# Top-k attention and a mixer MLP on one core: the distance to a candidate threshold as whole numbers, and weights that load later

## The chip, the cores and the metric

The kernel runs on one core of a Trainium2 chip. The time is the device time of one execution in microseconds (us). A core has five engines that run side by side, each through its own list of instructions in order: TensorE (PE, matrix products), VectorE (DVE), ScalarE (ACT), GpSimd (POOL) and SyncE (SP, which here only issues transfers). They wait for each other through semaphores. Sixteen DMA engines carry the transfers.

## The reference

```python
# q, k, v: (8, 8, 576, 64) float32;  x: (8, 576, 512)
scores = scale * np.matmul(q, k.transpose(0, 1, 3, 2))          # 576 x 576 per head
kth = np.partition(scores, -32, axis=-1)[..., -32:-31]          # 32nd largest of each row
scores = np.where(scores >= kth, scores, -1e9)
attn = softmax(scores);  attn_out = np.matmul(attn, v)
x = attn_out.transpose(0, 2, 1, 3).reshape(B, S, H * D)
h = np.maximum(x.transpose(0, 2, 1) @ w_tok1, 0.0) @ w_tok2     # token mixing, 576 -> 256 -> 576
u = x + h.transpose(0, 2, 1)
out = u + np.maximum(u @ w_ch1, 0.0) @ w_ch2                    # channel mixing, 512 -> 1536 -> 512
```

So each of 36,864 rows needs its own threshold, the 32nd largest of 576 scores, before its softmax.

## The kernel before

**Tiling.** Two heads make a pair; there are 32 pairs, four to a batch. The 576 rows of a head are four blocks of 128 and a rest of 64. For each pair, four groups `g` hold one block of both heads (two row tiles, `n == 2`), and a fifth group holds the two rests as one row tile. That gives 9 row tiles for a pair, 36 for a batch and 288 in all. Line numbers are those of the kernel before.

**One group.** Q and K are loaded by SyncE, transposed on TensorE (L369, L371) and copied out by ScalarE (L377, L380). Then:

1. TensorE multiplies the scores into PSUM (L399, L391); ScalarE copies them to `Sb` in SBUF (L429, L432).
2. VectorE takes the eight largest of each of seven segments of a row into `cd` (L442). Two rounds of maximum and replacement drop 16 values (L447 to L452), and the last maximum (L454) gives `thi`, whose eighth value is a candidate: at least 24 scores of the row are at or above it, in most rows exactly 24.
3. ScalarE's sign operation (L455) compares all 576 scores with the candidate, writes the signs to `sg`, and sums them into `cnt`, which tells the candidate's rank.
4. GpSimd multiplies scores and signs into `X` (L461): scores at or above the candidate become negative, those below stay positive. Eight dummy columns behind the 576 (L464, from `kdum` and `cnt`) stand for the places that the rank leaves, large or small, so that the eighth largest of the 584 columns is the threshold whatever the rank is between 24 and 31.
5. VectorE takes that maximum (L469, `tlo`), GpSimd negates its eighth value (L472, `nt`).
6. For groups of two, GpSimd writes the mask `U` as steep bytes from `Sb` and `nt` (L478). TensorE computes the scores a second time (L409) and adds the mask through the identity (L414); ScalarE's exponential writes `Pm` (L483). The single tile goes through `E`, `M` and a product on GpSimd instead (L488 to L493).
7. SyncE issues a DMA transpose `PT` (L497). When a pair's five groups have theirs and `vb`, V cast to bf16 by GpSimd (L382), is there, TensorE multiplies by V (L514, L518), and VectorE normalises into `Xb` (L530 to L539).

**MLP.** When a batch's four pairs are normalised, TensorE runs the MLP of that batch (first L562, then L580 to L589, L606, L627, L631) with copies on ScalarE (L569, L595, L612, L638). It runs between the attention of the next batch; the last batch's stands alone at the end.

**Order.** A planner in the kernel's source, `Plan`, writes every engine's order when the program is built. Each step is added with its engine, a duration and a due time; due times come from `T` (the spacing of row tiles) and the offsets `DUE`. A step is taken when its inputs, a free buffer and its engine are there in the planner's own account, no more than `AHEAD` before it is due. The order is then fixed: an engine that waits for one instruction does not pass to the next. Loads of weights are steps of GpSimd (`weight`, L307), which issues those transfers; all other transfers are issued by SyncE.

**Guard.** At the end `judge` (L662) tests counts and thresholds on VectorE; where a test fails, an exact version of the whole computation follows.

Of the kernel before, what the change touches and what calls it, by code (L numbers as in the profile page):

```python
# [8 lines left out]
P = 128  # L9
TOPK = 32  # L10
NEG = -1.0e30
LOW = -(2.0**100)
CUT = 8396807.0 / 8388608.0
NSEG = 7
RANK_BASE = 24
NDUM = 8
SHRINK = 2.0**-20
STEEP = -(2.0**100)
DROP = 2.0**-100
BELOW = -(1.0 - 2.0**-24)  # L20
FLOOR = 2.0**-66
# [3 lines left out]
T = 2.4326  # L25
DUE = dict(
    lq=30.233, tq=-12.175, ck=20.425, vc=11.748, mm=-33.047, cp=-28.9818283514137, seg=23.504, rnd=-2.208,
    sg=37.023, x=39.168, dum=4.693, mx=25.934, nt=-6.127, u=-3.8878283514136998, re=10.162, ex=-7.834,
    ex1=-1.811, tr=-27.916, pv=44.427, nm=-12.844, mlp=20.353,
# [10 lines left out]
class Op:  # L40
    __slots__ = ("eng", "dur", "due", "fn", "deps", "acq", "use", "lat", "n", "start", "end", "kids", "wait", "ready", "dma")


class Plan:
    LAT = {"DVE": 0.14, "ACT": 0.15, "POOL": 0.11, "PE": 0.13, "SP": 0.05}
    AHEAD = 87.6
# [8 lines left out]
    def add(self, eng, dur, due, fn, deps=(), acq=(), use=(), lat=None, dma=0.0):  # L55
# [5 lines left out]
        o.dma = dma  # L61
        o.n, o.kids = len(self.ops), []
# [27 lines left out]
    def run(self):  # L90
# [3 lines left out]
        for o in self.ops:  # L94
            o.wait, o.ready = len(o.deps), 0.0
# [87 lines left out]
def kernel(  # L183
# [14 lines left out]
    i32 = mybir.dt.int32  # L198
    u8 = mybir.dt.uint8
# [38 lines left out]
    lift = sbt("lift", [P, 1], f32)  # L238
    kdum = sbt("kdum", [P, NDUM], f32)
# [7 lines left out]
    tlo = sbt("tlo", [P, NT, 8], f32)  # L247
# [7 lines left out]
    slots("Sb", 5, [P, 2, S], f32)  # L255
# [3 lines left out]
    slots("sg", 4, [P, S], bf16)  # L259
    slots("X", 3, [P, 2, XW], f32)  # L260
# [4 lines left out]
    slots("PT", 9, [P, 10, P], bf16)  # L265
# [23 lines left out]
    for j in range(NDUM):  # L289
        nc.vector.memset(kdum[:, j : j + 1], float(S - 2 * RANK_BASE + 1 - 2 * (j + 1)))  # L290
# [10 lines left out]
    nc.vector.memset(lift[:, :], LIFT)  # L301
    for t in Xbs:
        nc.vector.memset(t[:, 4, :], 0.0)
# [3 lines left out]
    def weight(key, at, lat, f):  # L307
        wl.setdefault(key, []).append(plan.add("POOL", 1.0, at, f, lat=lat))
# [19 lines left out]
    def pair_ops(p):  # L328
# [6 lines left out]
        def ld_main(buf, src):  # L335
            for h in range(2):
                nc.sync.dma_start(
# [11 lines left out]
        def ld_kv(buf, src):  # L349
            def f():  # L350
                ld_main(buf, src)
                nc.sync.dma_start(
# [6 lines left out]
        lq = plan.add("SP", 0.24, tl, ld_q, acq=[qL], dma=1.4)  # L359
        lk = plan.add("SP", 0.2, tl + 0.1, ld_kv(kL, k), acq=[kL], dma=1.4)  # L360
        lv = plan.add("SP", 0.2, tl + 0.2, ld_kv(vL, v), acq=[vL], dma=1.4)
# [3 lines left out]
        def tr(buf, src, n):  # L365
# [11 lines left out]
        eq = plan.add("ACT", 0.62, t0 + DUE["ck"], lambda: nc.scalar.activation(  # L377
            out=qT.t[:, :], in_=pq.t[0][:, pq.t[1] : pq.t[1] + PW], func=AF.Copy, scale=SHRINK),
# [39 lines left out]
        for g in range(5):  # L418
# [17 lines left out]
            sgn, xs, mxs = [], [], []  # L436
            for h in range(n):
                i = i0 + h
                cd, m8, sg = Buf("cd"), Buf("m8"), Buf("sg")
                ss = []  # L440
                for a in range(NSEG):
# [13 lines left out]
                sgn.append(plan.add("ACT", 0.82, t + DUE["sg"] + 0.8 * h, lambda i=i, h=h, sg=sg, Sb=Sb: nc.scalar.activation(  # L455
                    out=sg.t[:, :], in_=Sb.t[:, h, :], func=AF.Sign, scale=-CUT, bias=thi[:, i, 7:8],
                    accum_out=cnt[:, i : i + 1]), [a5], acq=[sg], use=[Sb], lat=0.17))
                xs.append((i, h, sg))
            xo = []
            for i, h, sg in xs:  # L460
                xo.append(plan.add("POOL", 1.26, t + DUE["x"] + 1.4 * h, lambda h=h, sg=sg, Sb=Sb, X=X: nc.gpsimd.tensor_tensor(  # L461
                    out=X.t[:, h, 0:S], in0=Sb.t[:, h, :], in1=sg.t[:, :], op=ALU.mult),
                    [sgn[h]], acq=[X] if h == 0 else [], use=[Sb, sg, X]))
            dm = plan.add("POOL", 0.20, t + DUE["dum"], lambda n=n, i0=i0, X=X: nc.gpsimd.tensor_tensor(  # L464
                out=X.t[:, 0:n, S:XW], in0=kdum[:, :].unsqueeze(1).to_broadcast([P, n, NDUM]),
                in1=cnt[:, i0 : i0 + n].unsqueeze(2).to_broadcast([P, n, NDUM]), op=ALU.subtract),
                [xo[0]] + sgn, use=[X])
            for i, h, sg in xs:
                mxs.append(plan.add("DVE", 0.69, t + DUE["mx"] + 1.2 * h, lambda i=i, h=h, X=X: nc.vector.max(  # L469
                    tlo[:, i, :], X.t[:, h, :]), [dm, xo[h]], use=[X]))  # L470
            lasts.extend(mxs)
            on = plan.add("POOL", 0.27, t + DUE["nt"], lambda n=n, i0=i0, nt=nt: nc.gpsimd.tensor_scalar(  # L472
                out=nt.t[:, 0:n], in0=tlo[:, i0 : i0 + n, 7], scalar1=-1.0 if n == 2 else BELOW,
                scalar2=None, op0=ALU.mult), mxs, acq=[nt])
            if n == 2:
                us = []
                for i, h, sg in xs:
# [404 lines left out]
```

## Time and profile before

| | |
|---|---|
| median of 3 runs | 851.89 us (851.38 to 853.02) |
| the profiled execution, its own time | 854.5 us |
| its span, first to last instruction | 852.6 us |
| busy: PE, DVE, ACT, POOL | 772.0, 745.8, 680.8, 709.4 us |
| mean granted TensorE clock | 0.978 |

A row of instructions in the profile gives line, engine, operation, output and input with their shapes, the count, the busy time in us and the mean of one in ns, and then how long the engine stood idle just before them and for whom. A row of a stretch of time gives, for each engine, its busy time in that stretch and, in brackets, the number of instructions; then the granted TensorE clock as a share of full speed, the DMA engines' share and GB/s. A row of waits names who waited for whom: us in total, times, the longest. A row of a timeline gives the start and the length in us, and at its end the idle time before it with what released it. A row of DMA issues ends with the median time from issue to landing.

### The profile page before, as it was taken

The page shows a single profiled execution, that of the slowest core. Times are in us where ns is not written, and L with a number is a line of the kernel's source. Part 1 is how long each engine was busy: PE and PEld are TensorE (multiplying, and loading weights), DVE is VectorE, ACT ScalarE, POOL GpSimd, SP SyncE. Part 2 cuts the span into 40 slices and gives each one's busy share as a digit, 9 for nine tenths or more (in the row PEclk, how much of TensorE's full clock was granted, in tenths as well). Part 3 has the DMA queues.
Part 4 walks back from the last instruction along what each step waited for, and adds up shares of the span by engine and source line. Part 5 has one row for each costly group of instructions (what it writes and reads, how often), then busy time and mean ns, then how long its engine had stood idle before and what let it go on. Part 6 is the DMA issues. An engine that isn't in the chain of part 4 may idle for free.

```text
span 852.6 us, 20703 instructions
## 1 busy us (share of the span) xinstructions
PE 772.0 (91%) x6188; PEld 499.9 (59%) x6226; DVE 745.8 (87%) x4527; ACT 680.8 (80%) x1121; POOL 709.4 (83%) x978
## 2 busy tenths in 40 slices
PE   2467777999999999999999999999999999999995
PEld 1334445666566755676567755676567755676562
DVE  4499999999989998999989998999989998999700
ACT  1477777988789988899789988899789988898451
POOL 3299998999998999899988999899988999899500
PEclk9879988999999999999999999999999999999999
DMA  8945455456465555745486556755475555532701
GB/s 153 175 76 101 97 109 106 91 111 87 112 144 96 104 104 131 136 84 104 101 148 101 104 107 136 128 84 104 100 147 103 105 105 135 88 61 49 142 2 60
DMA packets 313017, 90.16 MB, mean 106 GB/s; under 512 B 305728, under 2 KB 307648, under 8 KB 312896
## 3 DMA queue, kind: packets, MB, share of 16 engines
q1 hardware_dynamic: 310144, 84.98, 51.5%
q0 software_dynamic: 2752, 3.77, 2.7%
q8 instruction: 51, 0.84, 0.4%
q14 instruction: 70, 0.57, 0.2%
HBM read 35.85 MB, written 9.44 MB: 53 GB/s over the span
## 4 chain that ended last, share of the span: by engine, by line
PE 52%; DVE 24%; POOL 8%; ACT 7%; issue 3%; DMA 3%; SPq 1%; ACTq 0%; POOLq 0%; DVEq 0%
PE bank L627 12%; PE bank L409 10%; DVE cd L442 9%; PE bank L399 7%; DVE tlo L469 7%; PE bank L606 6%; PE bank L414 5%; POOL X L461 3%; ACT Sb L429 3%; PE bank L514 3%; PE bank L369 2%; PE bank L391 2%; POOL U L478 2%; DMA vL<-in_v_dram 2%; ACT sg L455 2%
## 5 line engine op out<-in xcount | busy, mean ns | idle before, releaser
L442 DVE MAX8 cd<-Sb 128x8 f32<-128x82 f32 (+1 forms) x2016 | 393.0, 231 | 28.5 <-ACT Sb L429 28.2
L461 POOL TENSOR_TENSOR X<-Sb,sg 128x576 f32<-128x576 f32 x288 | 364.7, 1280 | 4.1 <-ACT sg L455 3.1
L455 ACT ACTIVATE sg<-Sb,thi 128x576 bf16<-128x576 f32 x288 | 222.8, 775 | 49.1 <-DVE thi L454 46.1
L469 DVE MAX8 tlo<-X 128x8 f32<-128x584 f32 x288 | 218.9, 761 | 21.8 <-POOL X L464 15.7
L478 POOL TENSOR_SCALAR U<-Sb,nt 128x576 uint8<-128x576 f32 x256 | 191.3, 747 | 23.8
L399 PE MATMUL bank<-kT,qT 64*128 64x288 f32 x1024 | 159.6, 438 | 24.7 <-ACT kT L380 13.4
L409 PE MATMUL bank<-kT,qT 64*128 64x288 f32 x1024 | 162.9, 437 | 7.8 <-ACT Sb L429 3.4
L483 ACT ACTIVATE Pm<-bank 128x1152 bf16<-128x1152 f32 x128 | 143.9, 1125 | 25.4 <-PE bank L414 21.0
L429 ACT COPY Sb<-bank 128x1152 f32<-128x1152 f32 x128 | 141.1, 1111 | 23.2 <-PE bank L399 20.8
L399 PEld LDWEIGHTS bank<-kT,qT 64*128 64x128 f32 x1024 | 91.9, 191 | 62.8 <-ACT Sb L429 15.7
L409 PEld LDWEIGHTS bank<-kT,qT 64*128 64x128 f32 x1024 | 93.9, 192 | 55.9 <-ACT Sb L429 11.2
L627 PE MATMUL bank<-wc2b,H 128*128 128x512 bf16 (+1 forms) x457 | 111.9, 380 | 2.8 <-issue 1.0
L606 PE MATMUL bank<-UT,wc1b 128*128 128x288 bf16 x768 | 104.3, 286 | 1.5 <-ACT UT L595 0.8
L414 PE MATMUL bank<-U,identN 128*128 128x288 bf16 x512 | 86.8, 292 | 10.5 <-POOL U L478 10.5
L606 PEld LDWEIGHTS <-wc1b 128*128 128x128 bf16 x768 | 73.5, 98 | 24.0 <-issue 5.0
L414 PEld LDWEIGHTS <-identN 128*128 128x128 bf16 x512 | 40.1, 98 | 69.0 <-issue 61.2
L627 PEld LDWEIGHTS <-H 128*128 128x128 bf16 (+1 forms) x480 | 45.3, 100 | 52.3 <-issue 8.2
L612 ACT ACTIVATE H<-bank 128x576 bf16<-128x576 f32 x96 | 61.6, 649 | 9.4 <-PE bank L606 7.8
L454 DVE MAX8 thi<-cd 128x8 f32<-128x56 f32 x288 | 58.5, 203 | 0.6
L455 ACT ACTIVATION_READ_ACCUMULATOR sg<-Sb,thi 128x1 f32 x288 | 55.6, 193 | 0.0
L450 DVE MAX8 m<-cd 128x8 f32<-128x35 f32 x288 | 52.6, 183 | 1.3
L452 DVE MATCH_REPLACE8 cd<-m,cd 128x35 f32<-128x35 f32 x288 | 52.6, 182 | 0.0
(85 smaller groups left out, 905.9 us busy)
## 6 DMA issues: line engine op xcount, KB each, us to landing
qL<-in_q_dram SPq DMA_DIRECT2D x64, 128.0 KB, 2.9
kL<-in_k_dram SPq DMA_DIRECT2D x64, 128.0 KB, 2.8
vL<-in_v_dram SPq DMA_DIRECT2D x64, 128.0 KB, 2.9
out_dram<-ob SPq DMA_DIRECT2D x16, 512.0 KB, 3.2
PT<-Pm SPq DMA_TRANSPOSE x160, 3.4
wc1b<-in_moe_w_ch_dram POOLq DMA_DIRECT2D x4, 384.0 KB, 9.0
wc2b<-in_moe_w_ch_dram POOLq DMA_DIRECT2D x4, 384.0 KB, 8.4
qL<-in_q_dram SPq DMA_DIRECT2D x64, 16.0 KB, 2.3
```

The lines of the kernel that those rows point to most:

```text
L399: nc.tensor.matmul(out=o[:, h, i, :], lhsT=qT.t[r, g * P : (g + 1) * P], rhs=kT.t[r, i * HS : (i + 1) * HS], start=True, stop=True)
L409: nc.tensor.matmul(out=o[:, h, i, :], lhsT=qT.t[r, g * P : (g + 1) * P], rhs=kT.t[r, i * HS : (i + 1) * HS], start=True, stop=False)
L414: nc.tensor.matmul(out=o[:, h, i, :], lhsT=identN[:, :], rhs=um[:, h, i * HS : (i + 1) * HS, 0], start=False, stop=True)
L429: nc.scalar.copy(out=Sb.t[:, :, :].rearrange("p h (a b) -> p h a b", a=2), in_=pairs(s1.t))
L442: ss.append(plan.add("DVE", 0.146, t + DUE["seg"] + 1.0 * h, lambda a=a, h=h, cd=cd, Sb=Sb: nc.vector.max(cd.t[:, a, :], Sb.t[:, h, bounds ...
L455: sgn.append(plan.add("ACT", 0.82, t + DUE["sg"] + 0.8 * h, lambda i=i, h=h, sg=sg, Sb=Sb: nc.scalar.activation(out=sg.t[:, :], in_=Sb.t[: ...
L461: xo.append(plan.add("POOL", 1.26, t + DUE["x"] + 1.4 * h, lambda h=h, sg=sg, Sb=Sb, X=X: nc.gpsimd.tensor_tensor(out=X.t[:, h, 0:S], in0= ...
L469: mxs.append(plan.add("DVE", 0.69, t + DUE["mx"] + 1.2 * h, lambda i=i, h=h, X=X: nc.vector.max(tlo[:, i, :], X.t[:, h, :]), [dm, xo[h]], ...
L478: us.append(plan.add("POOL", 0.80, t + DUE["u"] + 0.01 * h, lambda h=h, nt=nt, U=U, Sb=Sb: nc.gpsimd.tensor_scalar(out=U.t[:, h, :, 1], in ...
L483: oe = plan.add("ACT", 1.08, t + DUE["ex"], lambda s2=s2, Pm=Pm: nc.scalar.activation(out=Pm.t[:, :, 0:S].rearrange("p h (a b) -> p h a b" ...
L606: nc.tensor.matmul(out=o[:, i, :], lhsT=wc1b[:, cc, fc * P : (fc + 1) * P], rhs=UT.t[:, cc, i * HS : (i + 1) * HS], start=(cc == 0), stop= ...
L627: nc.tensor.matmul(out=po, lhsT=H2.t[:, fc, cs], rhs=wc2b[:, fc, :], start=(fc == 0), stop=False)
```

## The change

- `X` is now 32-bit whole numbers: score minus candidate, times `GRID` (2^34), by one scalar operation on GpSimd that reads `Sb` and the candidate. Scores below the candidate become negative.
- VectorE reads `X` as unsigned words, in which the negative numbers are the largest, so its maximum picks the scores next below the candidate.
- The sign now reads `X` and so comes after it, and writes one scratch tile `sg` instead of one of four; its sum `cnt` has the other sign, so `kdum` has too. The dummies of each row tile are an operation of their own.
- The masks are written from `X` instead of `Sb`. `Sb` has four buffers instead of five, `X` five instead of three, `PT` eight instead of nine.
- Q is no longer scaled when it is copied.
- A weight load is not planned before its due time (`nb`). K of the first pair is loaded through ScalarE's queue.
- The planner's durations, offsets, `T` and `AHEAD` are others, so all orders are written anew; the guard's tests are put in terms of the new numbers.

```diff
-T = 2.4326
+T = 2.3874
 DUE = dict(
...
-    AHEAD = 87.6
+    AHEAD = 196.0
...
-            o.wait, o.ready = len(o.deps), 0.0
+            o.wait, o.ready = len(o.deps), o.nb
...
-    slots("Sb", 5, [P, 2, S], f32)
+    slots("Sb", 4, [P, 2, S], f32)
...
-    slots("sg", 4, [P, S], bf16)
-    slots("X", 3, [P, 2, XW], f32)
+    sg = sbt("sg", [P, S], bf16)
+    slots("X", 5, [P, 2, XW], i32)
...
-    slots("PT", 9, [P, 10, P], bf16)
+    slots("PT", 8, [P, 10, P], bf16)
...
-        wl.setdefault(key, []).append(plan.add("POOL", 1.0, at, f, lat=lat))
+        wl.setdefault(key, []).append(plan.add("POOL", 0.6, at, f, lat=lat, nb=at))
...
-        lq = plan.add("SP", 0.24, tl, ld_q, acq=[qL], dma=1.4)
-        lk = plan.add("SP", 0.2, tl + 0.1, ld_kv(kL, k), acq=[kL], dma=1.4)
+        lq = plan.add("SP", 2.6, tl, ld_q, acq=[qL], dma=0.9)
+        lk = plan.add("SP", 1.9, tl + 0.1, ld_kv(kL, k, nc.scalar if p == 0 else nc.sync), acq=[kL], dma=0.9)
...
-                sgn.append(plan.add("ACT", 0.82, t + DUE["sg"] + 0.8 * h, lambda i=i, h=h, sg=sg, Sb=Sb: nc.scalar.activation(
-                    out=sg.t[:, :], in_=Sb.t[:, h, :], func=AF.Sign, scale=-CUT, bias=thi[:, i, 7:8],
-                    accum_out=cnt[:, i : i + 1]), [a5], acq=[sg], use=[Sb], lat=0.17))
...
-                xo.append(plan.add("POOL", 1.26, t + DUE["x"] + 1.4 * h, lambda h=h, sg=sg, Sb=Sb, X=X: nc.gpsimd.tensor_tensor(
-                    out=X.t[:, h, 0:S], in0=Sb.t[:, h, :], in1=sg.t[:, :], op=ALU.mult),
-                    [sgn[h]], acq=[X] if h == 0 else [], use=[Sb, sg, X]))
-            dm = plan.add("POOL", 0.20, t + DUE["dum"], lambda n=n, i0=i0, X=X: nc.gpsimd.tensor_tensor(
-                out=X.t[:, 0:n, S:XW], in0=kdum[:, :].unsqueeze(1).to_broadcast([P, n, NDUM]),
-                in1=cnt[:, i0 : i0 + n].unsqueeze(2).to_broadcast([P, n, NDUM]), op=ALU.subtract),
-                [xo[0]] + sgn, use=[X])
...
+                xo.append(plan.add("POOL", 0.77, t + DUE["x"] + 0.8 * h, lambda i=i, h=h, Sb=Sb, X=X: nc.gpsimd.tensor_scalar(
+                    out=X.t[:, h, 0:S], in0=Sb.t[:, h, :], scalar1=thi[:, i, 7:8], scalar2=GRID,
+                    op0=ALU.subtract, op1=ALU.mult), [a5], acq=[X] if h == 0 else [], use=[Sb, X]))
+                sgn.append(plan.add("ACT", 0.76, t + DUE["sg"] + 0.8 * h, lambda i=i, h=h, X=X: nc.scalar.activation(
+                    out=sg[:, :], in_=X.t[:, h, 0:S], func=AF.Sign, scale=1.0, bias=half[:, :],
+                    accum_out=cnt[:, i : i + 1]), [xo[h]], use=[X], lat=0.17))
+            for h in range(n):
+                dm = plan.add("POOL", 0.20, t + DUE["dum"] + 0.8 * h, lambda i=i0 + h, h=h, X=X: nc.gpsimd.tensor_scalar(
+                    out=X.t[:, h, S:XW], in0=kdum[:, :], scalar1=cnt[:, i : i + 1], scalar2=None,
+                    op0=ALU.subtract), [sgn[h]], use=[X])
+                mxs.append(plan.add("DVE", 0.69, t + DUE["mx"] + 1.2 * h, lambda i=i0 + h, h=h, X=X: nc.vector.max(
+                    tlo[:, i, :], X.t[:, h, :].bitcast(u32)), [dm, xo[h]], use=[X]))
...
-                    us.append(plan.add("POOL", 0.80, t + DUE["u"] + 0.01 * h, lambda h=h, nt=nt, U=U, Sb=Sb: nc.gpsimd.tensor_scalar(
-                        out=U.t[:, h, :, 1], in0=Sb.t[:, h, :], scalar1=nt.t[:, h : h + 1], scalar2=STEEP,
+                    us.append(plan.add("POOL", 0.80, t + DUE["u"] + 0.01 * h, lambda h=h, nt=nt, U=U, X=X: nc.gpsimd.tensor_scalar(
+                        out=U.t[:, h, :, 1], in0=X.t[:, h, 0:S], scalar1=nt.t[:, h : h + 1], scalar2=STEEP,
```

More of the change, by code (lines that the diff above doesn't have):

```diff
@@ L61, in add @@
         o.dma = dma
+        o.nb = nb
         o.n, o.kids = len(self.ops), []
@@ L198 @@
     i32 = mybir.dt.int32
+    u32 = mybir.dt.uint32
     u8 = mybir.dt.uint8
@@ L246 @@
     thi = sbt("thi", [P, NT, 8], f32)
-    tlo = sbt("tlo", [P, NT, 8], f32)
+    tlo = sbt("tlo", [P, NT, 8], u32)
+    tli = tlo.bitcast(i32)
     qLs = slots("qL", 2, [P, 5, 2, D], f32)
@@ L471, in pair_ops @@
             lasts.extend(mxs)
[L472 to L474 removed]
+            on = plan.add("POOL", 0.30, t + DUE["nt"], lambda n=n, i0=i0, nt=nt: nc.gpsimd.tensor_scalar(
+                out=nt.t[:, 0:n], in0=tli[:, i0 : i0 + n, 7], scalar1=-1.0,
+                scalar2=SLACK, op0=ALU.mult, op1=ALU.add), mxs, acq=[nt])
```

81 lines of the change are left out of this document (37 added, 44 removed).

## The prediction, made before the changed kernel ran

> **What bounds the kernel now.** I read the page's busy shares first, then the busy time of each engine stage by stage, and only then the waits. The page gives one execution:
>
> ```profile
> span 852.6 us, 20703 instructions
> PE 772.0 (91%) x6188; PEld 499.9 (59%) x6226; DVE 745.8 (87%) x4527; ACT 680.8 (80%) x1121; POOL 709.4 (83%) x978
> ```
>
> Four engines are above 80%, so the shares alone decide nothing. I cut the span at the first matmul of a batch's MLP (L562), because that is where TensorE gets a second kind of work. These rows show the cuts: the first MLP, the second, the seventh and the eighth.
>
> ```profile
> 148.30 0.22 PE bank L562
> ...
> L562 PE MATMUL bank<-Xb,w1b x9: 379/379/379, 254.3 to 256.3; 128*128 128x512 bf16 x9
> ...
> L562 PE MATMUL bank<-Xb,w1b x9: 379/379/379, 734.3 to 736.2; 128*128 128x512 bf16 x9
> ...
> 809.62 2.32 PE L562 MATMUL bank<-Xb,w1b 128*128 128x512 bf16 x9 [1.09 <-DVE Xb L532]
> ```
>
> The table of stages, with those cuts (the sixth row is one of the five equal periods between 254.3 and 734.3):
>
> ```profile
> core 0: us, PE busy (x) PEld busy (x) DVE busy (x) ACT busy (x) POOL busy (x), PEclk, DMA share, GB/s
> 22.70:50.00 27.30, 11.91 (x62) 7.45 (x60) 16.06 (x117) 13.31 (x23) 12.84 (x17) 0.75 0.80 140
> 50.00:100.00 50.00, 38.96 (x304) 24.24 (x300) 49.38 (x309) 39.46 (x66) 47.09 (x65) 0.93 0.56 103
> 100.00:148.30 48.30, 35.02 (x270) 22.10 (x268) 44.94 (x277) 35.57 (x59) 43.34 (x61) 0.86 0.51 100
> 148.30:254.30 106.00, 101.70 (x818) 65.83 (x821) 100.45 (x608) 92.68 (x152) 99.52 (x136) 1.00 0.56 109
> 638.30:734.20 95.90, 94.41 (x775) 61.43 (x779) 91.08 (x562) 84.70 (x141) 87.66 (x121) 1.00 0.57 113
> 734.30:809.60 75.30, 73.49 (x635) 48.40 (x638) 68.31 (x383) 58.65 (x97) 60.90 (x85) 1.00 0.43 81
> 809.60:852.60 43.00, 32.38 (x221) 20.39 (x223) 1.21 (x5) 13.98 (x20) 0.00 (x0) 0.95 0.09 30
> ```
>
> The reader should see three regimes. Stage A, up to 148.3, is attention alone: TensorE is idle a quarter of the time and VectorE carries it (49.38 of 50). From 148.3 on TensorE is busy 94.41 of every 95.9 us, at a granted clock of 1.00: it bounds the periods, with 1.5 us to spare, and VectorE (91.08) is close behind. The last 43.0 us are the last MLP. GpSimd, which the change relieves most, bounds no stage: it has 8 us to spare per period.
>
> **The fill.** Where VectorE stood still in stage A, and what stood behind it:
>
> ```profile
> DVE tlo L469 <- POOL X L464: 11.4, 2, 11.2
> DVE cd L442 <- ACT Sb L429: 9.7, 1, 9.7
> ```
>
> ```profile
> 12.47 0.55 DVE L303 MEMSET Xb<- 128x256 uint32 x2
> 17.07 1.09 PE L369 MATMUL bank<-identF,kL 128*128 128x128 f32 x4 [9.09 <-DMA kL<-in_k_dram]
> 22.68 1.27 DVE L442 MAX8 cd<-Sb 128x8 f32<-128x82 f32 x8 [9.66 <-ACT Sb L429]
> 31.11 0.72 POOL L382 TENSOR_SCALAR vb<-vL 128x640 bf16<-128x640 f32 x1 [9.78 <-DMA vL<-in_v_dram]
> 40.25 0.72 POOL L382 TENSOR_SCALAR vb<-vL 128x640 bf16<-128x640 f32 x1 [5.57 <-DMA vL<-in_v_dram]
> ```
>
> ```profile
> q0 software_dynamic: 1008, 1.80, 51.7%
> kL<-in_k_dram SPq DMA_DIRECT2D x4, 128.0 KB, 7.5
> vL<-in_v_dram SPq DMA_DIRECT2D x3, 128.0 KB, 12.0
> ```
>
> ```profile
> kL<-in_k_dram SPq DMA_DIRECT2D x64, 128.0 KB, 2.8
> vL<-in_v_dram SPq DMA_DIRECT2D x64, 128.0 KB, 2.9
> 0.74 1.36 SPq L337 DMA_DIRECT2D qL<-in_q_dram  x2
> ```
>
> In the first 20 us the weights (q0) take 51.7% of the DMA engines, and K and V need 7.5 and 12.0 us to land where 2.8 and 2.9 are the medians of the whole run. VectorE is through its memsets at 13.02 and waits for scores until 22.68. Then GpSimd stands at the V casts until 40.25 with the dummies (L464) queued behind it, and VectorE loses 11.2 us more.
>
> **Part by part.** The weights leave the start: in the new written order the first weight load stands behind the fourth X operation of GpSimd and the last behind the thirty-fifth. Pair 0's K goes to ScalarE's queue. Each issue takes 0.68 us (1.36 for two), so its three are out by 2.8 and, at 2.8 to 7.5 us, land at 5.6 to 10.3. From K's first transpose to VectorE's first maximum the rows give 22.68 - 17.07 = 5.6 us: 11.2 to 15.9. The memsets (one more, of one column) end at about 13.1, so VectorE starts at 13.1 to 15.9; I take 13.1, since the load of the DMA engines that made 7.5 is gone. The Trainium skill ("DMA: Bandwidth & Descriptors", "Issuing engines are not separate DMA queues") speaks against the move to ScalarE's queue: it saves issue time only. By it alone K would be out on SyncE at 5.4, land at 8.2, and the start be 13.8: the sum would be 0.7 worse. No run shows it yet.
>
> The V casts stay on GpSimd's path. SyncE's sixteenth issue (pair 1's V) ends at 0.74 + 16 x 0.68 = 11.6 and lands at 14.5; GpSimd needs it after two X, near 16. Its twenty-sixth (pair 2's V) lands at 18.4 + 2.9 = 21.3, behind the fifth X, near 22. So the 11.2 goes. If V still needs 12.0, the third lands at 30.4 and some 9 us of stall stay.
>
> Stage A also holds one tile's first part less: VectorE's written order has 44.7 row tiles' segments before the fourth normalisation, where before it had 45.7, and 40 last maxima in both. A tile is 91.08 / 36 = 2.53 us, of which the last maximum takes 0.76, so 1.77 for the rest.
>
> ```profile
> L461 POOL TENSOR_TENSOR X<-Sb,sg 128x576 f32<-128x576 f32 x288 | 364.7, 1280 | 4.1 <-ACT sg L455 3.1
> L469 DVE MAX8 tlo<-X 128x8 f32<-128x584 f32 x288 | 218.9, 761 | 21.8 <-POOL X L464 15.7
> L478 POOL TENSOR_SCALAR U<-Sb,nt 128x576 uint8<-128x576 f32 x256 | 191.3, 747 | 23.8
> L464 POOL TENSOR_TENSOR X<-kdum,cnt 128x16 f32<-128x16 f32 (+1 forms) x160 | 34.4, 215 | 12.1 <-ACT sg L455 4.6
> ```
>
> Stage A after: 13.1 + (148.3 - 22.7) - 11.2 - 1.8 = 125.7, **22.6 us earlier**. Bounds: 25 earlier if VectorE's other idle time shrinks too; 10.8 earlier if it starts at 15.9 and 9 us of stall stay.
>
> GpSimd's own saving: X becomes one scalar operation with one tile read. The nearest row is the mask (747 ns; same width, scalar operand per row); the far end is the old 1280. At 747 a period saves 36 x 0.533 = 19.2 us, and pays 16 more dummy operations x 0.215 = 3.4: GpSimd goes from 87.66 to 71.9. That is worth nothing directly, since TensorE ends the periods. Twelve weight issues move between the X operations; at most 9.4 us in all, hidden by that slack:
>
> ```profile
> L311 POOL DMA_DIRECT2D wc2b<-in_moe_w_ch_dram x4 | 3.1, 780 | 0.0
> ```
>
> The sign moves behind X, on ScalarE. It now writes one scratch tile, so each sign waits for the one before; behind it in ScalarE's queue are the copies out of PSUM, for which TensorE waits. What is lost is this overlap:
>
> ```profile
> 29.38 0.19 ACT L455 ACTIVATION_READ_ACCUMULATOR sg<-Sb,thi 128x1 f32 x1
> 29.47 0.76 ACT L455 ACTIVATE sg<-Sb,thi 128x576 bf16<-128x576 f32 x1
> ```
>
> The second sign starts 0.10 before the first one's sum is read out (29.57). Lost 36 times a period, that is 3.6 us: ScalarE 84.70 to 88.3 of 95.9. I charge TensorE 0.4 of it per period, bounds 0 and 3.6. The Trainium skill ("ScalarE: Activation LUTs", "What ACT_TABLE_LOAD costs") says that back-to-back activations overlap by about 93 ns, which this row agrees with; by that figure 288 signs would cost 27 us if all of it lay on the path, which is the slower rival below. VectorE's maximum over unsigned words I leave at 761 (+0 to +0.1). The scaling of Q and the checks at the end change no count that matters.
>
> Stage B (148.3 to 254.3): TensorE's written order has 27, 50, 70 ... 160 score blocks before the eight MLPs in both kernels, so its work stays 101.70. VectorE's falls: 35.3 tiles begun and 37 finished, before 39.3 and 42: 4 x 1.77 + 5 x 0.76 = 10.9 less, 89.6. So TensorE with the periods' idle ends it: 101.7 + 1.5 = 103.2; I take 103.5, **2.5 earlier** (0 to 4.3).
>
> Five periods: 480.0 + 5 x 0.4: **2 later** (7.5 earlier, with no idle left, to 10 later).
>
> Stage D (734.3 to 809.6): those tiles come back. VectorE has 27 tiles to begin and 29 to finish, before 22.7 and 27: 4.3 x 1.77 + 2 x 0.76 = 9.1 more, 77.4 against 75.3. So at least 2.1 later, at most 9.1; **I take 4**, as 7 us of its idle time are there to fill. The last MLP stays at 43.0.
>
> Sum: -22.6 - 2.5 + 2 + 4 = -19.1. The profiled execution took 854.5 (852.6 of span), which becomes 835.4; the median of the runs, 851.89, becomes **832.8**.
>
> **The rivals.** *GpSimd still stands at V*: the loads' rate, not the weights, sets V's landing. Then A gains 10.8: 844.6. For it: the loads of three pairs still stand in a row on SyncE. Against: 51.7% of the DMA time was the weights'. 0.12. *TensorE reaches its floor*: with GpSimd's slack every period is 94.4: 2 + 7.5 less, 823.3; 0.10. *X is no cheaper*: the conversion holds it at 1280 ns; GpSimd is at 87.66 + 3.4 = 91.1 a period, which still fits, but its masks come later; at 1 us a period 840; 0.05. *Slower, through ScalarE*: the sign waits for GpSimd and for the sign before it, with the PSUM copies queued behind it. If none of the 3.6 is hidden, 6.8 periods from B to D pay 24.5 instead of the 2: 855.3. It decides from 3.0 us a period, where the 20 us gained are spent. For it: ScalarE's 11 us of slack are in small pieces. Against: the copies have TensorE's own pace to hide in. 0.12. *Slower, through VectorE*: unsigned words cost 0.1 per maximum, 3.6 a period, VectorE 94.7 against TensorE's 94.4; nearly all 8 batches pay: 860; 0.03.
>
> **How the numbers follow.** My forecast has 0.58. The bounds of A, C and D taken together reach from 817 to 860; 819 to 851 leaves out the two slower cases and little else. What a measurement of this kernel can tell from no change is 0.2%, 1.7 us. Faster: 0.58 + 0.10 + most of 0.12 and 0.05 = 0.83; the same 0.02; slower 0.15.
>
> **What would show it.** Right: VectorE's first maximum near 13, no wait of 11 us at the dummies, X near 750 ns, the first L562 near 126, periods of 96, and the stretch from the seventh to the eighth MLP near 79. Wrong: a first L562 after 138 (the V casts), periods over 97 with ScalarE's copies late (the signs), a last maximum over 0.8 us.

## The result, and the profile after

The changed kernel takes **1240.34 us** (median of 4 runs, 1239.87 to 1241.34), the kernel before 851.63 us (849.22 to 853.02) beside it: ratio 1.457, 95% interval 1.4535 to 1.4605. The prediction said 832.8 us, 819 to 851. It was wrong in sign and by some 400 us.

The page of the changed kernel, its span and busy times, and then the chain that ended last, by engine and by line:

```profile
span 1238.2 us, 20908 instructions
PE 902.9 (73%) x6226; PEld 561.9 (45%) x6226; DVE 748.9 (60%) x4527; ACT 690.4 (56%) x1121; POOL 1044.1 (84%) x1106
...
POOL 53%; DVE 24%; issue 11%; PE 8%; ACT 3%; DMA 0%; POOLq 0%; ACTq 0%
POOL X L459 33%; DVE cd L446 10%; POOL U L478 9%; DVE tlo L469 8%; POOL X L466 5%; PE bank L627 2%; POOL nt L472 2%; POOL Pm L493 1%; DVE cd L456 1%; ACT Sb L433 1%; PE bank L606 1%; DVE cd L452 1%; POOL vb L386 1%; PE bank L413 1%; PE bank L403 1%
```

GpSimd was to fall from 709.4 us of work; it has 1044.1, and the chain runs through it. The costliest groups of the same page say why:

```profile
L459 POOL TENSOR_SCALAR X<-Sb,thi 128x576 int32<-128x576 f32 x288 | 639.4, 2220 | 45.5 <-DVE thi L458 19.3
L469 DVE MAX8 tlo<-X 128x8 uint32<-128x584 uint32 x288 | 217.8, 767 | 422.0 <-POOL X L466 420.1
L462 ACT ACTIVATE sg<-X,half 128x576 bf16<-128x576 int32 x288 | 223.4, 776 | 393.7 <-POOL X L459 393.1
...
L478 POOL TENSOR_SCALAR U<-X,nt 128x576 uint8<-128x576 int32 x256 | 191.3, 747 | 23.5
...
L466 POOL TENSOR_SCALAR X<-kdum,cnt 128x8 int32<-128x8 f32 x288 | 88.7, 311 | 25.8 <-ACT sg L462 7.7
```

X takes 2220 ns, where the mask, an instruction of the same name, width and kind of operands, takes 747. Against the 747 of the prediction that is 288 x 1.473 = 424 us more work for GpSimd; the span is 1238.2 - 833.5 = 405 us longer than forecast (833.5 is the old span less the 19.1 of the sum). VectorE stands still for 422.0 us before the last maximum and ScalarE for 393.7 before the sign, nearly all of it for X and its dummies (L466). The stages, cut at the first matmul of an MLP as before (the first attention, then the stretch from the first to the second MLP, one period from the fourth to the fifth, the stretch from the seventh to the eighth, the end):

```profile
50.00:100.00 50.00, 31.37 (x218) 20.78 (x218) 29.13 (x186) 27.60 (x45) 46.48 (x49) 0.76 0.52 94
...
187.40:350.50 163.10, 121.22 (x823) 74.31 (x823) 102.51 (x626) 93.68 (x153) 146.60 (x155) 0.87 0.37 71
644.30:790.50 146.20, 110.95 (x781) 69.42 (x780) 91.72 (x560) 86.08 (x140) 129.38 (x137) 0.87 0.38 75
1083.90:1195.60 111.70, 83.74 (x640) 53.25 (x638) 69.49 (x381) 59.87 (x99) 89.34 (x97) 0.91 0.30 54
1195.60:1238.20 42.60, 32.57 (x226) 20.41 (x224) 0.76 (x3) 14.58 (x21) 0.00 (x0) 0.96 0.10 34
```

A period lasts 146.2 us, where it was 95.9. In it VectorE and ScalarE do what they did (91.72 against 91.08, 86.08 against 84.70); GpSimd does 129.38 instead of 87.66, and is the fullest. TensorE runs the same matmuls more slowly (110.95 for 781, before 94.41 for 775): its granted clock is 0.87 where it was 1.00. Only the last MLP, without GpSimd, is as long as before.

One group's selection in the timeline of the changed kernel (GpSimd, VectorE and ScalarE):

```profile
705.12 0.31 POOL L466 TENSOR_SCALAR X<-kdum,cnt 128x8 int32<-128x8 f32 x1
705.46 0.77 DVE L469 MAX8 tlo<-X 128x8 uint32<-128x584 uint32 x1 [1.57 <-POOL X L466]
705.51 4.54 POOL L459 TENSOR_SCALAR X<-Sb,thi 128x576 int32<-128x576 f32 x2
...
707.77 0.77 ACT L462 ACTIVATE sg<-X,half 128x576 bf16<-128x576 int32 x1 [2.24 <-POOL X L459]
...
708.45 0.19 ACT L462 ACTIVATION_READ_ACCUMULATOR sg<-X,half 128x1 f32 x1
...
710.08 0.77 ACT L462 ACTIVATE sg<-X,half 128x576 bf16<-128x576 int32 x1 [0.91 <-POOL X L459]
710.14 0.31 POOL L466 TENSOR_SCALAR X<-kdum,cnt 128x8 int32<-128x8 f32 x1
710.49 0.77 DVE L469 MAX8 tlo<-X 128x8 uint32<-128x584 uint32 x1 [2.65 <-POOL X L466]
```

Two X in a row hold GpSimd for 4.54 us. The sign of the first follows at 707.77 and is summed by 708.64, but the next dummies come only when both X are through, at 710.14, and VectorE has stood 2.65 us before its last maximum at 710.49.

### The profile page after: what moved, and what is told of

It reads as the page before. It is cut to its first block, busy times and chain, and to the rows that moved or that the text cites. A ratio compares the mean times of both kernels' runs of the same rounds, so it can differ in the third digit from the quotient of the medians.

```text
span 1238.2 us, 20908 instructions
## 1 busy us (share of the span) xinstructions
PE 902.9 (73%) x6226; PEld 561.9 (45%) x6226; DVE 748.9 (60%) x4527; ACT 690.4 (56%) x1121; POOL 1044.1 (84%) x1106
## 4 chain that ended last, share of the span: by engine, by line
POOL 53%; DVE 24%; issue 11%; PE 8%; ACT 3%; DMA 0%; POOLq 0%; ACTq 0%
POOL X L459 33%; DVE cd L446 10%; POOL U L478 9%; DVE tlo L469 8%; POOL X L466 5%; PE bank L627 2%; POOL nt L472 2%; POOL Pm L493 1%; DVE cd L456 1%; ACT Sb L433 1%; PE bank L606 1%; DVE cd L452 1%; POOL vb L386 1%; PE bank L413 1%; PE bank L403 1%
## 5 line engine op out<-in xcount | busy, mean ns | idle before, releaser
L459 POOL TENSOR_SCALAR X<-Sb,thi 128x576 int32<-128x576 f32 x288 | 639.4, 2220 | 45.5 <-DVE thi L458 19.3
L469 DVE MAX8 tlo<-X 128x8 uint32<-128x584 uint32 x288 | 217.8, 767 | 422.0 <-POOL X L466 420.1
L462 ACT ACTIVATE sg<-X,half 128x576 bf16<-128x576 int32 x288 | 223.4, 776 | 393.7 <-POOL X L459 393.1
L403 PE MATMUL bank<-kT,qT 64*128 64x288 f32 x1024 | 184.6, 490 | 91.1 <-ACT Sb L433 42.6
L413 PE MATMUL bank<-kT,qT 64*128 64x288 f32 x1024 | 193.7, 482 | 66.8 <-ACT Pm L483 25.0
L478 POOL TENSOR_SCALAR U<-X,nt 128x576 uint8<-128x576 int32 x256 | 191.3, 747 | 23.5
L403 PEld LDWEIGHTS bank<-kT,qT 64*128 64x128 f32 x1024 | 105.4, 218 | 145.2 <-ACT Sb L433 53.4
L413 PEld LDWEIGHTS bank<-kT,qT 64*128 64x128 f32 x1024 | 109.1, 216 | 131.2 <-ACT Pm L483 38.0
L466 POOL TENSOR_SCALAR X<-kdum,cnt 128x8 int32<-128x8 f32 x288 | 88.7, 311 | 25.8 <-ACT sg L462 7.7
L514 PE MATMUL bank<-vb,PT 128*128 128x65 bf16 x1280 | 56.8, 213 | 35.2 <-ACT Pm L483 33.2
L514 PEld LDWEIGHTS <-PT 128*128 128x128 bf16 x1280 | 54.0, 111 | 43.8 <-issue 39.4
L472 POOL TENSOR_SCALAR nt<-tlo 128x2 f32<-128x2 int32 (+1 forms) x160 | 30.7, 192 | 33.5 <-DVE tlo L469 18.2
```

The source lines that it names most:

```text
L403: nc.tensor.matmul(out=o[:, h, i, :], lhsT=qT.t[r, g * P : (g + 1) * P], rhs=kT.t[r, i * HS : (i + 1) * HS], start=True, stop=True)
L413: nc.tensor.matmul(out=o[:, h, i, :], lhsT=qT.t[r, g * P : (g + 1) * P], rhs=kT.t[r, i * HS : (i + 1) * HS], start=True, stop=False)
L459: xo.append(plan.add("POOL", 0.77, t + DUE["x"] + 0.8 * h, lambda i=i, h=h, Sb=Sb, X=X: nc.gpsimd.tensor_scalar(out=X.t[:, h, 0:S], in0=Sb ...
L462: sgn.append(plan.add("ACT", 0.76, t + DUE["sg"] + 0.8 * h, lambda i=i, h=h, X=X: nc.scalar.activation(out=sg[:, :], in_=X.t[:, h, 0:S], f ...
L466: dm = plan.add("POOL", 0.20, t + DUE["dum"] + 0.8 * h, lambda i=i0 + h, h=h, X=X: nc.gpsimd.tensor_scalar(out=X.t[:, h, S:XW], in0=kdum[: ...
L478: us.append(plan.add("POOL", 0.80, t + DUE["u"] + 0.01 * h, lambda h=h, nt=nt, U=U, X=X: nc.gpsimd.tensor_scalar(out=U.t[:, h, :, 1], in0= ...
```

## The experiments

**What makes X dear?** Five things are new around the instruction: the whole-number output, the unsigned reader, numbers too large for 32 bits, the subtraction, the order of the instructions around it. A small kernel without the computation ran six of each form on 128 x 576:

```python
nc.gpsimd.tensor_scalar(out=f_i32, in0=src, scalar1=thr[:, 0:1], scalar2=GRID, op0=ALU.subtract, op1=ALU.mult)
# the same into f32, u32, u8, int16, bf16; with ALU.add; over 288 columns; on VectorE
```

> A kernel of its own that measures single operations on 128x576 tiles (six of each; nothing of the reference is computed, the output is zeros). X's operation took 2220 ns where the mask, also a scalar operation with a per-row operand, took 747. Theory 'output': what costs is that GpSimd writes 32-bit whole numbers from float32. Then subtract-and-multiply into float32 takes about 750 ns and into bf16 and bytes about 750, into int32 about 2220, add-and-multiply into int32 also about 2220, and whole numbers in, float32 out, about 750. Theory 'operation': subtracting a per-row operand is the slow part; then the float32 output takes 2220 too, and add-and-multiply into int32 750. Theory 'range': numbers beyond 32 bits are the slow part; then add-and-multiply by 2^20 into int32, all in range, takes 750. With 288 columns into int32, theory 'output' expects (2220 - 311) / 568 = 3.36 ns per column, so about 1250 ns; a fixed cost would leave it above 1900. Eight columns: about 310 into int32, 190 to 215 into float32.

Groups of instructions by line (subtraction into float32, into int32, into uint8; 288 columns; addition into int32; VectorE's subtraction):

```profile
L63 POOL TENSOR_SCALAR f_f<-src,thr 128x576 f32<-128x576 f32 x6 | 13.3, 2213 | 3.1 <-DMA src<-in_q_dram 2.6
L65 POOL TENSOR_SCALAR f_i<-src,thr 128x576 int32<-128x576 f32 x6 | 13.3, 2212 | 0.5
...
L69 POOL TENSOR_SCALAR f_u<-src,thr 128x576 uint8<-128x576 f32 x6 | 13.3, 2210 | 0.5
...
L77 POOL TENSOR_SCALAR g_i<-src,thr 128x288 int32<-128x288 f32 x6 | 7.5, 1250 | 0.5
...
L75 POOL TENSOR_SCALAR g_i<-src,thr 128x576 int32<-128x576 f32 x6 | 4.5, 745 | 0.5
...
L93 DVE TENSOR_SCALAR d_i<-g_f,thr 128x576 int32<-128x576 f32 x6 | 4.2, 705 | 122.1 <-POOL g_f L91 122.1
```

Same price into every type; with the addition in place of the subtraction, a third of it, into whole numbers as well. The type is out, and so is the size of the numbers, since float32 costs as much. The whole kernel says the same (its maximum reads float32 too, so the unsigned reader is gone from it):

```diff
-    tlo = sbt("tlo", [P, NT, 8], u32)
+    tlo = sbt("tlo", [P, NT, 8], f32)
-    slots("X", 5, [P, 2, XW], i32)
+    slots("X", 5, [P, 2, XW], f32)
```

> The changed kernel with X in float32 instead of int32 (tile, maximum and all readers); its order of instructions is the same, one for one. The selection is then not that of the reference, and the guard's verdict is left out. If the 2220 ns of X are the whole cause and the rest of the prediction holds: X near 750 ns, first MLP matmul near 126 us, periods near 96, the stretch from the seventh to the eighth MLP near 79, and 833 us in all (819 to 851). Rival 'order': the new orders and the sign behind X cost by themselves; then it stays well above 852, with periods over 99 us.

1242.13 us, ratio 1.4544 (1.4499 to 1.4589), X at 2222 ns: nothing changes. It stays above 852 us, as the run's rival had it, but by X's price and not by the orders alone. Is it then the subtraction? A second small kernel took other operations:

> Which operation of a GpSimd scalar operation is slow; 128x576 float32 in, int32 out, six of each, nothing of the reference computed. So far subtract-and-multiply took 2210 ns into all six output types, and add-and-multiply 745 into int32 and float32: the theory 'output' is out, 'operation' stands. New theory 'subtract': every scalar operation with a subtraction in it is slow, wherever it stands and with a per-row or a constant operand. Then 1500 to 2300 for subtract alone, subtract with a constant, and multiply-and-subtract, 750 or less for add alone, multiply-and-add, add-and-add. Rival 'common pairs': only add and multiply are fast and all else is slow: then also maximum, and greater-or-equal take over 1500. Tensor minus tensor: if the subtraction itself were slow, above 1280; 1280 if only the scalar form is. Eight columns with add: about 200 instead of 306; one column times -1: about 190.

Its groups by line, in this order: subtraction and multiplication; subtraction alone; addition alone; multiplication then addition; multiplication then subtraction; two additions; two multiplications:

```profile
L64 POOL TENSOR_SCALAR f_i<-src,thr 128x576 int32<-128x576 f32 x6 | 13.3, 2212 | 2.2 <-DMA src<-in_q_dram 1.8
...
L66 POOL TENSOR_SCALAR f_i<-src,thr 128x576 int32<-128x576 f32 x6 | 10.3, 1722 | 0.0
...
L72 POOL TENSOR_SCALAR f_i<-src,thr 128x576 int32<-128x576 f32 x6 | 10.3, 1723 | 0.6
...
L74 POOL TENSOR_SCALAR f_i<-src,thr 128x576 int32<-128x576 f32 x6 | 4.5, 745 | 0.6
...
L76 POOL TENSOR_SCALAR f_i<-src,thr 128x576 int32<-128x576 f32 x6 | 13.3, 2212 | 0.6
L78 POOL TENSOR_SCALAR f_i<-src,thr 128x576 int32<-128x576 f32 x6 | 13.3, 2210 | 0.6
...
L86 POOL TENSOR_SCALAR f_i<-src,thr 128x576 int32<-128x576 f32 x6 | 4.5, 745 | 0.6
```

So "the subtraction is slow" falls too: an addition alone costs 1723, two additions 2210, and between two tensors subtraction and multiplication cost the same (1395 and 1396). Three pairs were cheap, addition with multiplication in either order and two multiplications; every other scalar operation tried on 576 columns (a maximum or a comparison with a multiplication, 2208 and 2209, among them) was not. The rows of all these forms read alike; only the source tells them apart.

**Is X's price the whole loss?** In the changed kernel only the operation of X, and so the selection, was altered; the guard's verdict is left out:

```diff
-                    op0=ALU.subtract, op1=ALU.mult), [a5], acq=[X] if h == 0 else [], use=[Sb, X]))
+                    op0=ALU.add, op1=ALU.mult), [a5], acq=[X] if h == 0 else [], use=[Sb, X]))
```

> The changed kernel with one word different: X adds the candidate instead of subtracting it (the selection is then not the reference's, and the guard's verdict is left out). The order of instructions is the same, one for one, and X is still int32. Theory 'subtract': X at 745 to 760 ns and the time falls from 1240 to the range of the prediction, 833 (819 to 851). Rival 'order': the new orders cost too, and it stays above 852. By the prediction's steps: first MLP near 126, periods near 96, seventh to eighth MLP near 79.

843.38 us, ratio 0.9878 (0.9842 to 0.9914), in the prediction's range. With the order of every engine kept, this one word is worth 397 us. X's group, and then the stages with its own cuts (first to second MLP, fourth to fifth, seventh to eighth, end):

```profile
L459 POOL TENSOR_SCALAR X<-Sb,thi 128x576 int32<-128x576 f32 x288 | 214.5, 745 | 58.9 <-DVE thi L458 37.2 <-DMA qL<-in_q_dram 0.7
```

```profile
127.00:234.50 107.50, 102.69 (x823) 64.76 (x822) 101.70 (x626) 91.92 (x153) 86.81 (x156) 1.00 0.56 107
431.40:528.40 97.00, 95.53 (x781) 61.44 (x778) 90.84 (x562) 85.29 (x140) 76.18 (x137) 1.00 0.58 111
722.40:797.20 74.80, 73.96 (x640) 48.16 (x639) 66.13 (x364) 57.78 (x96) 51.28 (x92) 1.00 0.42 81
797.20:839.60 42.40, 32.54 (x226) 20.37 (x224) 0.74 (x3) 14.56 (x21) 0.00 (x0) 0.96 0.11 34
```

**How much of the loss is the order?** The planner had 0.77 us for X and 0.20 for the dummies; here it was told what they take:

```diff
-                xo.append(plan.add("POOL", 0.77, t + DUE["x"] + 0.8 * h, ...
+                xo.append(plan.add("POOL", 2.28, t + DUE["x"] + 0.8 * h, ...
-                dm = plan.add("POOL", 0.20, t + DUE["dum"] + 0.8 * h, ...
+                dm = plan.add("POOL", 0.32, t + DUE["dum"] + 0.8 * h, ...
```

> The changed kernel with the planner told what X and the dummies take (2.28 and 0.32 us instead of 0.77 and 0.20); the work of every engine is the same, only the order differs. If GpSimd's work is the cause by itself, its 1044 us of work, a last MLP of 43 and a start of 15 leave 1100 us at the least, and the time falls from 1240 to between 1110 and 1200. If the order made for a fast X is no part of the loss, it stays within 1% of 1240.

1207.35 us, ratio 1.4132 (1.4076 to 1.4188), a little over the 1110 to 1200 expected: 33 us of the loss are the order that a cheap X was planned for. The rest stays. GpSimd's waits for other engines between the first MLP and the last, and the busy times of that stretch:

```profile
POOL X L466 <- ACT sg L462: 2.6, 5, 0.9
POOL nt L472 <- DVE ones L663: 0.9, 1, 0.9
...
180.60:1163.60 983.00, 776.44 (x5379) 478.60 (x5379) 684.87 (x3808) 596.06 (x961) 894.66 (x939) 0.84 0.37 73
```

GpSimd waits 3.5 of 983.0 us, though it counts as busy for only 894.66: the rest lies between its instructions, mostly some 0.09 us from the end of one to the start of the next. So it is full and sets the time. In the changed kernel's own order it waited 45.5 of 1010.2 us in the same stretch.

**What are the other parts worth?** The kernel before, with `nb` and the weights' 0.6 us, and pair 0's K on ScalarE's queue; the next two runs do one of these each.

```diff
-            o.wait, o.ready = len(o.deps), 0.0
+            o.wait, o.ready = len(o.deps), o.nb
-        wl.setdefault(key, []).append(plan.add("POOL", 1.0, at, f, lat=lat))
+        wl.setdefault(key, []).append(plan.add("POOL", 0.6, at, f, lat=lat, nb=at))
-        lk = plan.add("SP", 0.2, tl + 0.1, ld_kv(kL, k), acq=[kL], dma=1.4)
+        lk = plan.add("SP", 0.2, tl + 0.1, ld_kv(kL, k, nc.scalar if p == 0 else nc.sync), acq=[kL], dma=1.4)
```

> The kernel before with two parts of the change alone: a weight load is not planned before its due time, and K of the first pair goes through ScalarE's queue. X, sign and dummies are as before. If the prediction's reading of the fill holds, VectorE's first maximum comes at 13 us instead of 22.7, the wait of 11.2 us at the dummies goes, the first MLP starts some 15 to 22 us earlier, and the time falls to 830 to 838. Rival: later in the run TensorE's fixed work gives it back, and the time falls by less than 8 us.

842.78 us, ratio 0.9863 (0.9833 to 0.9893). VectorE's first maximum in the timeline, its longest waits in the first 150 us, and a period:

```profile
12.94 1.20 DVE L443 MAX8 cd<-Sb 128x8 f32<-128x82 f32 x8
```

```profile
DVE tlo L470 <- POOL X L462: 3.5, 4, 1.3
DVE tlo L470 <- POOL X L465: 3.4, 6, 1.9
```

```profile
434.70:530.70 96.00, 94.84 (x780) 61.44 (x779) 91.30 (x562) 84.72 (x140) 87.94 (x121) 1.00 0.62 112
```

The stalls of 9.7 and 11.2 us are gone, the first MLP starts at 135.6 instead of 148.1, and the period is as before. Neither expected case was met: the first MLP comes 12.5 us earlier, not 15 to 22, and the time falls by 11.1 us, neither to 830 to 838 nor by less than 8. Weights late, K left on SyncE:

> The kernel before with the weights loaded late, and with pair 0's K left on SyncE's queue; the version that also moves K to ScalarE's queue took 842.8 us (ratio 0.986 to the kernel before). If the late weights are what shortens the start, K lands some 2 us later at most, VectorE's first maximum starts at 12.9 to 14.5, and the time lies at 840 to 845 us. If K's queue is needed, the first maximum starts after 16 and the time lies at 846 to 851 us.

844.26 us, ratio 0.9919 (0.9894 to 0.9944); the first maximum starts at 12.93, the first MLP at 138.0, 2.4 later than with K on ScalarE's queue: the third V cast starts at 22.65 instead of 21.14, since K's three issues, some 2 us, now stand ahead of V's on SyncE. Only K moved, the weights at the start:

> The kernel before with pair 0's K on ScalarE's queue and nothing else: the weights still load at the start. If the weights' traffic is what delays K and V, VectorE's first maximum still starts at 18 to 23, its wait of 11 us at the dummies stays, and the time lies at 847 to 853 us. If the order of issues on SyncE was the cause, both go and the time lies at 840 to 845 us.

850.9 us, ratio 0.9987 (0.9965 to 1.0009): no change that can be told. The first maximum's row and VectorE's longest waits in the first 150 us:

```profile
15.91 1.26 DVE L442 MAX8 cd<-Sb 128x8 f32<-128x82 f32 x8 [2.89 <-ACT Sb L429]
```

```profile
DVE tlo L469 <- POOL X L464: 14.6, 2, 14.4
```

Both theories of that run missed the start, which lay between them, at 15.9. Of the 6.8 us that the start gains (22.68 to 15.91), 3.2 go again at the V casts (14.4 instead of 11.2); the first MLP starts at 144.3, 3.8 earlier. Only the late weights remove both stalls. One thing K's move alone did: K's first transpose started at 10.33 instead of 17.07, 6.7 us earlier, though K's issues ended only 2.6 us sooner (2.78 instead of 5.40).

Then the version with late weights was given SyncE's true issue times (as the changed kernel has for Q and K, and V, the transposes and the stores likewise):

```diff
-        lq = plan.add("SP", 0.24, tl, ld_q, acq=[qL], dma=1.4)
+        lq = plan.add("SP", 2.6, tl, ld_q, acq=[qL], dma=0.9)
-            od = plan.add("SP", 0.06, t + DUE["tr"], dt, [oe], acq=[PTb], use=[Pm], dma=2.0 if n == 2 else 1.1)
+            od = plan.add("SP", 1.36, t + DUE["tr"], dt, [oe], acq=[PTb], use=[Pm], dma=1.0 if n == 2 else 0.7)
```

> The kernel before with the weights loaded late and K through ScalarE (the version that took 842.8 us), and the planner told how long SyncE really takes to issue the DMAs. If the order that the planner writes out is still wrong for SyncE's queue, the period between the MLP marks (96.0 us in the version with late weights) becomes shorter and the time lies at 825 to 839 us. If VectorE sets the period whatever SyncE's order is, the time stays at 840 to 846 us.

840.9 us, ratio 0.9874 (0.9854 to 0.9895): the same as without. This order of SyncE does not shorten the period: 95.9 us from the fourth MLP to the fifth, 96.0 before.

**Can whole numbers be kept with a cheap pair?** The candidate is negated first, on GpSimd, and X is an addition and a multiplication; the sign changes its sense, and the dummies become a single addition:

```diff
+                ng = plan.add("POOL", 0.28, t + DUE["x"] + 0.8 * h, lambda i=i: nc.gpsimd.tensor_scalar(
+                    out=nth[:, i : i + 1], in0=thi[:, i, 7:8], scalar1=-1.0, scalar2=None, op0=ALU.mult), [a5])
-                    ... scalar1=thi[:, i, 7:8], scalar2=GRID, op0=ALU.subtract, op1=ALU.mult), [a5], ...
+                    ... scalar1=nth[:, i : i + 1], scalar2=GRID, op0=ALU.add, op1=ALU.mult), [ng], ...
```

> The whole computation, with the candidate's negative taken by one more small GpSimd operation per row tile (one column, about 0.2 us), then X by add-and-multiply and dummies by add. GpSimd: 1044 us less 288 x 1.47 for X, less 288 x 0.1 for the dummies, plus 288 x 0.2: about 650, below the 709 of the kernel before. Theory 'subtract': 830 to 845 us, faster than the kernel before. Rival 'order' as above: over 852.

879.02 us, ratio 1.0298 (1.026 to 1.0336): over 852, as the rival had it, and not the 830 to 845 of an X that is cheap at no other cost. With the negation on VectorE (`nc.vector.tensor_scalar`):

> As the one before, but VectorE negates the candidate right after its last maximum (one column, 60 to 150 ns there, 288 times, 17 to 43 us of VectorE's time, which is 91 of 96 us busy in a period). If VectorE has no room for it: 5 to 30 us slower than the GpSimd variant; if the shorter path to X counts for more: equal or up to 5 us faster.

864.67 us, ratio 1.0125 (1.0088 to 1.0162), 14.4 us less than with GpSimd's negation, where 5 less at most was expected. Whether the shorter path to X or GpSimd's relief makes it, the run does not separate. With the negation on GpSimd as a multiplication by -1 and an addition of 0, and the dummies as an addition and a multiplication by 1:

> The whole-number version with X as an addition and a multiplication (745 ns) and the negated candidate from an extra GpSimd operation, which took 879.0 us; here the dummies are an addition and a multiplication by 1, and the negation a multiplication by -1 and an addition of 0, so that every GpSimd operation in the chain of a selection is one of the pairs that were cheap at 576 columns. If the pair decides at 8 columns and at one as well, the dummies fall from 320 to some 200 ns and the negation from 224 to some 190, and the time lies at 850 to 870 us. If at so few columns a fixed cost decides, whatever the pair, the time stays at 875 to 882 us.

856.57 us, ratio 1.0056 (1.0039 to 1.0073). Its two short operations, and those of the version at 879.02 before it:

```profile
L469 POOL TENSOR_SCALAR X<-kdum,cnt 128x8 int32<-128x8 f32 x288 | 78.7, 277 | 25.5 <-ACT sg L465 8.7
L460 POOL TENSOR_SCALAR nth<-thi 128x1 f32<-128x1 f32 x288 | 55.1, 191 | 26.0 <-DVE thi L459 9.0 <-ACT Sb L434 6.9
```

```profile
L469 POOL TENSOR_SCALAR X<-kdum,cnt 128x8 int32<-128x8 f32 x288 | 91.4, 320 | 25.3 <-ACT sg L465 8.5
L460 POOL TENSOR_SCALAR nth<-thi 128x1 f32<-128x1 f32 x288 | 64.5, 224 | 25.9 <-DVE thi L459 16.0
```

A cheap pair helps at 8 columns and at one too, by 43 and 33 ns (the dummies stay at 277, not 200). That is 288 x 0.076 = 21.9 us of work, and the time fell by 22.5. GpSimd's busy share of 78% at 879.02 us hides how full it was: between the first MLP and the last it waited for others only 34.1 of 700.1 us, with 576.2 busy and the rest between its 1180 instructions. These operations also lie in the chain of a selection. Which of the two makes the 22.5 no run separates.

The stretch from the first to the last MLP matmul sums it up (L562, or the line it became in the version):

| version | first | last | between | GpSimd busy | median |
|---|---|---|---|---|---|
| before | 148.1 | 811.6 | 663.5 | 709.4 | 851.6 |
| late weights, K moved | 135.6 | 800.1 | 664.5 | 712.2 | 842.8 |
| after, X as an addition (another selection) | 127.0 | 799.1 | 672.1 | 618.2 | 843.4 |
| pairs throughout | 130.3 | 814.2 | 683.9 | 658.9 | 856.6 |
| negated on VectorE | 128.3 | 822.3 | 694.0 | 621.3 | 864.7 |
| negated on GpSimd | 134.2 | 834.3 | 700.1 | 681.3 | 879.0 |
| after | 187.4 | 1197.6 | 1010.2 | 1044.1 | 1240.3 |

Every whole-number form has a longer middle than the float product, though GpSimd's busy time is less in each but the last. What of it is the sign behind X, what the separate dummies, what the time between GpSimd's more numerous instructions, what the orders, no run separates.

## Why the prediction was wrong, step by step

- **X's price: the step that failed.** "The nearest row is the mask" at 747, "the far end is the old 1280"; measured 2220. The mask adds and multiplies, X subtracts and multiplies; the row names neither, and both are in the source. Width, types and operands were matched, the operation was not. The range's bounds were taken from rows of other operations, so they bounded nothing. With X's price fell the path: "TensorE ends the periods" holds at 745 ns (95.53 of 97.0 us busy in the version with the addition); at 2220 GpSimd ends them.
- **"GpSimd goes from 87.66 to 71.9"** a period: 129.38. X alone accounts for 36 x 1.473 = 53.0 of the 57.5 between; the dummies, taken at 215, took 311, 36 x 0.096 = 3.5 more.
- **The rival "X is no cheaper"** named the right place, GpSimd, but priced X at 1280, where GpSimd "still fits" its period, 840 us and 0.05. At 2220, GpSimd's 71.9 + 53.0 = 125 us a period exceed TensorE's 94.4, which the prediction's own table would have told. Neither slower rival (ScalarE, VectorE) was the way it went.
- **GpSimd's room was smaller than read.** The prediction's "it has 8 us to spare per period" takes all time that isn't busy as spare. Between the first MLP and the last of the kernel before, GpSimd waited for others 18.2 us in all, of 663.5 - 598.7 = 64.8 that weren't busy; the rest lay between its instructions.
- **The fill: right in its times.** The first maximum was put at 13.1, as early as the memsets allow, and starts at 12.94; the V casts no longer hold VectorE. In the changed kernel's timeline:

```profile
12.94 1.20 DVE L446 MAX8 cd<-Sb 128x8 f32<-128x82 f32 x8
```

- **K's queue: no matter at the start once the weights are late.** By the page "DMA: Bandwidth & Descriptors" of the Trainium skill, moving K saves issue time only, and by it the start with K on SyncE was worked out as 13.8. With late weights and K on SyncE it is 12.93: the memsets end it either way. The later V casts are issue time on SyncE, as the page has it (the third 1.5 us later for some 2 us of issues); the 0.7 worked out from it for the start does not show. With the weights at the start the measurement goes beyond the page: K's first transpose came 6.7 us earlier for 2.6 us of issue time. Why, no run shows.
- **Stage A, given a cheap X: right in size, by two misses of opposite sign.** 125.7 forecast, 127.0 in the version with the addition; 187.4 with X at 2220. Up to the first MLP, before and in that version:

```profile
0.00:148.30 148.30, 92.08 (x653) 58.12 (x654) 120.40 (x729) 92.08 (x152) 110.88 (x158) 0.88 0.63 117
0.00:127.00 127.00, 96.75 (x652) 61.32 (x653) 116.77 (x710) 90.07 (x147) 96.55 (x175) 0.87 0.80 136
```

VectorE's idle time fell by 17.7 us (27.9 to 10.2), where the two stalls were to give 9.6 + 11.2 = 20.8; its work fell by 3.6, where 1.8 was forecast.
- **Stages B and D: the count of tiles was wrong.** B was to hold 4 to 5 row tiles less on VectorE and D to get them back. In the version with the addition, whose written order is the changed kernel's, B holds 283 segment maxima and 41 last maxima, 40.4 tiles begun where 35.3 were forecast and 41 finished where 37 were; D holds 21.3 and 25 where 27 and 29 were. So VectorE works 101.70 us in B instead of 89.6, and 66.13 in D instead of 77.4: at the second MLP it had begun 85 tiles, not 80, and so nothing came back in D.
- **B, C, D, given a cheap X.** Forecast 103.5, 482, 79.3; the version with the addition has 107.5, 722.4 - 234.5 = 487.9, and 74.8. A gives 1.3 more than forecast, B 4.0, C 5.9, D 4.5 less, E 0.6 less: 839.6 against 833.5. "Five periods: 2 later" was the largest miss here: 7.9 later. That the sum is only 6.1 off is partly luck: misses of both signs lie in it. The signs' lost overlap is not seen in ScalarE's work: 85.29 us a period, before 84.70, where the prediction had 88.3. ScalarE's wait before the sign went from 15.0 to 21.5 us in the five periods; whether that makes the 7.9 was not tried by itself.
- **What gains: the late weights.** Of the 19.1 forecast, the late weights give 7.9 us with the float product kept, and 11.1 with K's queue (each against the kernel before beside it). What K's queue adds is not told clearly: the two medians, 844.26 and 842.78, are 1.5 apart. In the version with the addition the first MLP starts 8.6 us earlier still than with late weights and K moved, and 7.6 of these go again between the MLPs (672.1 against 664.5). "That is worth nothing directly" for GpSimd's relief fits this: with GpSimd at 76.18 us a period instead of 87.94, the period is 97.0 instead of 96.0.
- **The unsigned maximum: right.** 761 (+0 to +0.1 us) forecast, 767 measured.

## What to carry to other kernels

Price an operation by a row of the same operations in the source, not only of the same instruction, width and types: where there is none, bound it by measuring it, since six repeats in a small kernel would have told this one. An engine with slack becomes the bound when one of its instructions triples, so a rival should ask at what price the slack is gone (here 94.4 - 71.9 = 22.5 us a period, or 0.62 us more for each X, 1.37 in all). That is the latest point: with 0.09 us after each of the 137 instructions of a period, an estimate from the version with the planner told, some 12 of the 22.5 are gone before. Of a change with several parts, the part that frees the start was worth having by itself: late weights and K's queue, 842.8 us, and no version with whole numbers that makes the reference's selection was faster than 856.6.

## What the runs showed of the hardware

- GpSimd's scalar operation on 128 x 576: 745 ns for addition with multiplication in either order and for two multiplications, 2208 to 2213 for the other pairs with a scalar per row, 1721 to 1723 for one operation alone (addition, subtraction or comparison; a multiplication alone was not measured at this width). Such a single operation costs more than twice a cheap pair, so an added multiplication by 1 or addition of 0 can pay (320 to 277 ns at 8 columns, 224 to 191 at one).
- The type written made no difference to subtraction with multiplication: float32, int32, uint32, uint8, int16 and bfloat16 all take 2210 to 2213 ns. Addition with multiplication took 745 into float32 and int32.
- From 288 to 576 columns the slow pair goes from 1250 to 2212 ns, 3.34 ns a column. The Trainium skill ("GPSIMD Engine Reference", "Elementwise — side-by-side cycle accounting") gives about 1.8 cycles an element at 1.2 GHz as the best case of a tight unrolled loop, which would be an estimate of 864 ns here: the cheap pairs are faster than that, the others far slower. The page does not name these pairs. Why they differ no run shows.
- GpSimd can be full at a busy share of 91%: with the planner told, it waited 3.5 of 983.0 us and was busy 894.66; from the end of one instruction to the start of the next lay mostly some 0.09 us.
- A period's matmuls took 110.95 us of TensorE at a granted clock of 0.87 (781 on record) and 94.41 at 1.00 (775).
